# RWKV attention and a squared-ReLU FFN on one core: transposing the scaled r and k by DMA, and a second PSUM bank for FFN2

## The chip, the core and the metric

The kernel runs on one core of a Trainium2 chip. The core has a matrix engine (TensorE, PE in the profile, with its weight loads in a row of their own, PEld), three engines for elementwise work (VectorE, DVE; ScalarE, ACT; GpSimd, POOL), and SyncE (SP), which here only issues DMAs. Each engine takes its instructions in the order in which they were emitted and waits at each for what it needs. TensorE writes to PSUM, which has eight banks of 2 KB per partition; everything else lies in SBUF. DMAs are moved by 16 DMA engines and issued from SP's queue (SPq in the timeline).

The metric is the device time in microseconds of one execution. A profiled execution gives the trace that the text quotes.

## The reference

Two steps, cut to what is computed. `r`, `k`, `v` are (4, 8, 768, 48): batch, heads, time steps, head dimension.

```python
for t in range(S):                       # S = 768
    cur = einsum('bhd,bhe->bhde', u * k[t], v[t])
    y[:, :, t] = einsum('bhd,bhde->bhe', r[t], state + cur)
    state = w * state + einsum('bhd,bhe->bhde', k[t], v[t])
x = y.transpose(0, 2, 1, 3).reshape(3072, 384)
h = maximum(x @ w_in, 0)                 # w_in is 384 x 2048
out = (h * h) @ w_out                    # w_out is 2048 x 384
```

## The kernel before

**Chunks.** Time is cut into 6 chunks of 128 steps; with 4 batches that makes 24 chunks, numbered so that chunk i is time chunk i // 4 of batch i % 4. Inside a chunk the recurrence becomes matrix products. With k scaled by powers of w (`kh`) and r by their inverse counterpart (`rt`), the products of every pair of steps are A = kh times rt (transposed both), masked to the causal half and stored as `Bm`. Then Y = rt times the carried state plus Bm times v, and U = kh times v updates the state. The state of a batch is `S0W[b]`.

**Functions of a chunk.** `prep` (L201) multiplies k and r by the tables `Wkhat` and `Wt2` into `kh_buf` and `rt_buf`, four buffers each, in bf16, with heads padded from 48 to 64 columns. `prep_du` (L206) makes the product for the u term (`P`). `cast_v` (L213) casts v on ACT. `bonus` (L218) reduces P to `du` and multiplies it by v (`dv`) on DVE. `piece_T` (L229) transposes kh and rt on PE, eight transposes of 128 x 128 into one PSUM bank of pool `psT`, and one ACT copy (L239) brings them to SBUF as `rkT`. `piece_A` (L242) is eight matmuls on `rkT` into `Ap` and two DVE multiplications by the mask (L258). `piece_YU` (L261) is Y and U on PE, then `xs` = Y + dv (L288) and the state update: `ts` on DVE (L295), and `S0W` on POOL (L296). `piece_X` (L299) transposes xs on PE into a bank of `psT` and copies it to `xT` on ACT (L307).

**FFN.** Two chunks make a group g, of which there are 12. `piece_F1` (L312) computes 256 of the 2048 hidden columns for the 256 rows of a group: six matmuls into `hp` (pool `psH`, two banks), ReLU on ACT to `hr` (L326), and the square `hq` on DVE (L331), for every fourth piece on ACT (L329). The bank of `hp` is free when DVE has read it. `piece_F2` (L336) does four matmuls of one chunk's output into `o`, which lies in pool `psO` with one bank; after the fourth piece of a chunk, ACT copies it to `os` (L353) and SP stores it (L354).

**Order.** The order is written out by hand. `period(ga, g1, g2)` (L391) has eight steps; step s emits FFN1 piece s of group g1, FFN2 piece s of group g2 (steps 0 to 3 the first chunk, 4 to 7 the second), then the attention step of group ga (`att`, L356): T of the first chunk a at step 0, A of a and T of b at step 1, A of b at 2, Y and U at 3 and 4, X at 5 and 6. At step 7 the loads of chunks 2ga + 6 and 2ga + 7 are issued, from ga = 2 on `preps` (L379) emits the prep of the next group's chunks on POOL at steps 0, 2, 4 and 6. Two groups of attention go first, with prep on DVE; then the weights are cast on POOL, FFN1 of groups 0 and 1 runs alone, chunks 4 and 5 are prepared, and `period(2, None, 0)` follows. From then on each period holds attention of group g + 1, FFN1 of g and FFN2 of g - 1.

**PSUM.** The banks are psT 1, psA 2 (both halves of `Ap`), psY 1, psU 1, psH 2, psO 1: all eight.

Of the kernel before, what the change touches and what calls it, by code (L numbers as in the profile page):

```python
# [10 lines left out]
BF16 = mybir.dt.bfloat16  # L11
# [5 lines left out]
def kernel(  # L17
# [11 lines left out]
    nc = tc.nc  # L29

    B, H, S, D = r.shape
# [3 lines left out]
    DP = 64  # L35
    HP = H // 2
# [3 lines left out]
    CCH = d_model // 128  # L40
# [6 lines left out]
    const = ctx.enter_context(tc.tile_pool(name="const", bufs=1))  # L47
    stage = ctx.enter_context(tc.tile_pool(name="stage", bufs=3))
    loads = ctx.enter_context(tc.tile_pool(name="loads", bufs=7))
    work = ctx.enter_context(tc.tile_pool(name="work", bufs=3))  # L50
    hid = ctx.enter_context(tc.tile_pool(name="hid", bufs=3))

    psT = ctx.enter_context(tc.tile_pool(name="psT", bufs=1, space=bass.MemoryType.PSUM))
    psA = ctx.enter_context(tc.tile_pool(name="psA", bufs=1, space=bass.MemoryType.PSUM))
    psY = ctx.enter_context(tc.tile_pool(name="psY", bufs=1, space=bass.MemoryType.PSUM))
    psU = ctx.enter_context(tc.tile_pool(name="psU", bufs=1, space=bass.MemoryType.PSUM))
    psH = ctx.enter_context(tc.tile_pool(name="psH", bufs=2, space=bass.MemoryType.PSUM))
    psO = ctx.enter_context(tc.tile_pool(name="psO", bufs=1, space=bass.MemoryType.PSUM))

    def bcast_rows(src):  # L60
        return bass.AP(
# [13 lines left out]
    def load(i):  # L75
        if i >= N:
            return
        c, b = i // B, i % B
        rf = loads.tile([128, H, D], FP32, name=f"rf_{i}", tag="rf")
        kf = loads.tile([128, H, D], FP32, name=f"kf_{i}", tag="kf")  # L80
        vf = loads.tile([128, H, D], FP32, name=f"vf_{i}", tag="vf")
        nc.sync.dma_start(out=rf, in_=r_v[b, c])
        nc.sync.dma_start(out=kf, in_=k_v[b, c])
        nc.sync.dma_start(out=vf, in_=v_v[b, c])
        nat[i] = (rf, kf, vf)
# [18 lines left out]
    def cast_w2(s):  # L104
        t = const.tile([128, 2, d_model], BF16, name=f"W2_{s}")
        nc.gpsimd.tensor_copy(t, W2f[s])  # L106
        W2.append(t)
# [44 lines left out]
    njcol = const.tile([128, 1], FP32, name="njcol")  # L152
    nc.vector.tensor_copy(njcol, njcol_i)
    NB = 4
    rt_buf, kh_buf = [], []
    for j in range(NB):
        tr = const.tile([128, H, DP], BF16, name=f"rt_{j}")
        tk = const.tile([128, H, DP], BF16, name=f"kh_{j}")
        nc.vector.memset(tr[:, :, D:DP], 0.0)
        nc.vector.memset(tk[:, :, D:DP], 0.0)  # L160
        rt_buf.append(tr)
        kh_buf.append(tk)
    wrow = const.tile([1, 2, HP, 128], FP32, name="wrow")
    nc.vector.memset(wrow, 0.0)
    esel = const.tile([1, 2, 2 * D], FP32, name="esel")
# [34 lines left out]

    def prep(i, eng):  # L201
        rf, kf, vf = nat[i]
        eng.tensor_mul(kh_buf[i % NB][:, :, 0:D], kf, Wkhat)  # L203
        eng.tensor_mul(rt_buf[i % NB][:, :, 0:D], rf, Wt2)

    def prep_du(i, eng):  # L206
        rf, kf, vf = nat[i]
        P0 = work.tile([128, H, D], FP32, name=f"P0_{i}", tag="P0")
        eng.tensor_mul(P0, rf, kf)  # L209
        eng.tensor_mul(P0, P0, ub)  # L210
        du_in[i] = P0
# [14 lines left out]
        nc.vector.tensor_mul(dv, nat[i][2], du_b)  # L226
        dvs[i] = dv

    def piece_T(i):  # L229
        pt = psT.tile([128, 2, HP, 128], BF16, name=f"pt_{i}", tag="T")  # L230
        for j, src in ((1, kh_buf[i % NB]), (0, rt_buf[i % NB])):
            for hc in range(HP):
                nc.tensor.transpose(  # L233
                    pt[:, j, hc, :],
                    src[:, 2 * hc : 2 * hc + 2, :].rearrange("p a b -> p (a b)"),
                    identity,
                )
        rkT = work.tile([128, 2, HP, 128], BF16, name=f"rkT_{i}", tag="rkT")
        nc.scalar.copy(rkT, pt)  # L239
        rkTs[i] = rkT  # L240

    def piece_A(i):  # L242
        rkT = rkTs[i]
        Ap = psA.tile([128, 2, HP, 128], FP32, name=f"Ap_{i}", tag="A")
        Bm = work.tile([128, 2, HP, 128], BF16, name=f"Bm_{i}", tag="Bm")
        for hc in range(HP):
            for e in range(2):
                p0 = 64 * e
                nc.tensor.matmul(
                    Ap[:, e, hc, :],  # L250
                    rkT[p0 : p0 + D, 1, hc, :],
                    rkT[p0 : p0 + D, 0, hc, :],
                    start=True,
                    stop=True,
                    skip_group_check=True,
                )
        for e in range(2):
            nc.vector.tensor_mul(Bm[:, e], Ap[:, e], mask_b)  # L258
        Bms[i] = Bm

    def piece_YU(i):  # L261
        c, b = i // B, i % B
        rkT, Bm, vb = rkTs.pop(i), Bms.pop(i), vbs.pop(i)
        Y = psY.tile([128, HP, 2 * D], FP32, name=f"Y_{i}", tag="Y", padded_shape=[None, None, 128])
        for hc in range(HP):
            if c > 0:
                nc.tensor.matmul(
                    Y[:, hc, :], rkT[:, 0, hc, :], S0W[b][:, hc, :],
                    start=True, stop=False, skip_group_check=True,
                )  # L270
            for e in range(2):
                nc.tensor.matmul(
                    Y[:, hc, D * e : D * (e + 1)], Bm[:, e, hc, :], vb[:, 2 * hc + e, :],
                    start=(c == 0), stop=True, skip_group_check=True,
                )
        if c < NCH - 1:
            kh = kh_buf[i % NB]
            U = psU.tile([128, HP, 2 * D], FP32, name=f"U_{i}", tag="U", padded_shape=[None, None, 128])
            for hc in range(HP):
                nc.tensor.matmul(  # L280
                    U[:, hc, :],
                    kh[:, 2 * hc : 2 * hc + 2, :].rearrange("p a b -> p (a b)"),
                    vb[:, 2 * hc : 2 * hc + 2, :].rearrange("p a b -> p (a b)"),
                    start=True, stop=True, skip_group_check=True,
                )
        xs = work.tile([128, HP, 2 * D], BF16, name=f"xs_{i}", tag="xs")
        dv = dvs.pop(i)
        nc.vector.tensor_add(xs, Y, dv.rearrange("p (a e) d -> p a (e d)", e=2))  # L288
        xss[i] = xs
        if c < NCH - 1:  # L290
            if c == 0:
                nc.vector.tensor_mul(S0W[b], U, WLm)
            else:
                ts = work.tile([128, HP, 2 * D], FP32, name=f"ts_{i}", tag="ts")
                nc.vector.tensor_add(ts, U, S0W[b])  # L295
                nc.gpsimd.tensor_mul(S0W[b], ts, WLm)  # L296
        nat.pop(i)

    def piece_X(i):  # L299
        g, j = i // 2, i % 2  # L300
        if j == 0:
            xTs[g] = work.tile([128, CCH, GT], BF16, name=f"xT_{g}", tag="xT")
        xf = xss.pop(i).rearrange("p a b -> p (a b)")
        px = psT.tile([128, CCH, 128], BF16, name=f"px_{i}", tag="T", padded_shape=[None, 8, None])
        for c in range(CCH):
            nc.tensor.transpose(px[:, c, :], xf[:, 128 * c : 128 * (c + 1)], identity)  # L306
        nc.scalar.copy(xTs[g][:, :, L * j : L * (j + 1)], px)  # L307
# [48 lines left out]
    def att(g, s):  # L356
        a = 2 * g
        b = a + 1
        if s == 0:
            cast_v(a)  # L360
            piece_T(a)
            bonus(a)
        elif s == 1:
            piece_A(a)
            piece_T(b)
        elif s == 2:
            cast_v(b)
            piece_A(b)
            bonus(b)
        elif s == 3:  # L370
            piece_YU(a)
        elif s == 4:
            piece_YU(b)
        elif s == 5:
            piece_X(a)
        elif s == 6:
            piece_X(b)

    def preps(g, s):  # L379
        if g >= NG:  # L380
            return
        if s == 0:
            prep(2 * g, nc.gpsimd)
        elif s == 2:
            prep_du(2 * g, nc.gpsimd)
        elif s == 4:
            prep(2 * g + 1, nc.gpsimd)
        elif s == 6:
            prep_du(2 * g + 1, nc.gpsimd)

    def period(ga, g1, g2):  # L391
        for s in range(8):
            if g1 is not None:
                piece_F1(g1, s)
            if g2 is not None:
                piece_F2(g2, s)
            if ga is not None:
                att(ga, s)
                if s == 7:
                    load(2 * ga + 6)  # L400
                    load(2 * ga + 7)
                if ga > 1:
                    preps(ga + 1, s)

    for i in range(4):
        prep(i, nc.vector)
        prep_du(i, nc.gpsimd)
        if i % 2 == 1:
            period(i // 2, None, None)
    for s in range(NS):  # L410
        cast_w1(s)
    for s in range(NS):
        cast_w2(s)
    period(None, 0, None)
    period(None, 1, None)
    for i in (4, 5):
        prep(i, nc.gpsimd)
        prep_du(i, nc.gpsimd)
    period(2, None, 0)
    for g in range(2, NG + 1):  # L420
        period(g + 1 if g + 1 < NG else None, g if g < NG else None, g - 1)
# [30 lines left out]
```

## Time and profile before

| | us |
|---|---|
| median of 2 runs | 215.95 (215.7 to 216.2) |
| the profiled execution | 217.31 |
| its span in the trace | 215.6 |

| engine | busy, us |
|---|---|
| PE | 179.5 |
| DVE | 135.5 |
| ACT | 128.2 |
| POOL | 120.9 |

Busy time is the time in which an engine has an instruction in work; PE's matmuls overlap, so a busy PE is not one at its peak. The span falls into parts: the attention of the first four chunks until the first FFN1 piece at 33.2 us, FFN1 of two groups until about 51.5, a period with attention and FFN2 alone until 62.5, nine full periods of about 14.6 us until 194.5, one period of FFN1 and FFN2, and the last FFN2. The trace names its rows by tile with a running number (`rkT_1691`, `o_1940`) and the line of the kernel; "idle before" in square brackets at the end of a row is how long the engine had nothing to do before it, and what ended that time.

### The profile page before, as it was taken

The page shows a single profiled execution, that of the slowest core. Times are in us where ns is not written, and L with a number is a line of the kernel's source. Part 1 is how long each engine was busy: PE and PEld are TensorE (multiplying, and loading weights), DVE is VectorE, ACT ScalarE, POOL GpSimd, SP SyncE. Part 2 cuts the span into 40 slices and gives each one's busy share as a digit, 9 for nine tenths or more (in the row PEclk, how much of TensorE's full clock was granted, in tenths as well). Part 3 has the DMA queues.
Part 4 walks back from the last instruction along what each step waited for, and adds up shares of the span by engine and source line. Part 5 has one row for each costly group of instructions (what it writes and reads, how often), then busy time and mean ns, then how long its engine had stood idle before and what let it go on. Part 6 is the DMA issues. An engine that isn't in the chain of part 4 may idle for free.

```text
span 215.6 us, 4553 instructions
## 1 busy us (share of the span) xinstructions
PE 179.5 (83%) x1784; PEld 132.2 (61%) x1784; DVE 135.5 (63%) x234; ACT 128.2 (59%) x223; POOL 120.9 (56%) x130
## 2 busy tenths in 40 slices
PE   0853548677799999999999999999999999999963
PEld 0742335454476867767677677676677666676631
DVE  3389983445749749669389487594794864943300
ACT  4351405667356687575865875767758758765530
POOL 2486973995089593792873956928929930000000
PEclk9999999999999999999999999999999999999999
DMA  5999999996019238166093291480840010011101
GB/s 113 194 214 301 389 299 297 192 224 122 36 40 188 72 82 175 40 146 149 0 212 83 59 187 53 107 184 7 184 111 36 0 40 36 3 36 38 40 36 73
DMA packets 84021, 25.85 MB, mean 120 GB/s; under 512 B 75552, under 2 KB 84000, under 8 KB 84000
## 3 DMA queue, kind: packets, MB, share of 16 engines
q1 hardware_dynamic: 84000, 25.57, 49.2%
q8 instruction: 14, 0.23, 0.5%
q14 instruction: 7, 0.06, 0.1%
HBM read 20.84 MB, written 4.72 MB: 119 GB/s over the span
## 4 chain that ended last, share of the span: by engine, by line
PE 67%; ACT 13%; DVE 11%; issue 6%; DMA 2%; ACTq 0%
PE wl_ps L186 2%; DMA wb<-in_w_dram 2%; PE o_3324 L342 1%; PE o_3304 L342 1%; PE o_1675 L342 1%; PE o_2205 L342 1%; PE o_2470 L342 1%; PE o_1940 L342 1%; PE o_1410 L342 1%; PE o_1145 L342 1%; PE o_2960 L342 1%; PE o_3251 L342 1%; PE o_3187 L342 1%; PE o_3097 L342 1%; PE o_1295 L342 1%
## 5 line engine op out<-in xcount | busy, mean ns | idle before, releaser
L317 PEld LDWEIGHTS <-W_0_474 128*128 128x128 bf16 x72 | 7.3, 102 | 3.0 <-issue 0.9
L186 PE MATMUL wl_ps<-esel,wrow 1*128 1x96 f32 x16 | 3.7, 423 | 6.4 <-ACT wrow L178 6.4
L317 PEld LDWEIGHTS <-W_6_486 128*128 128x128 bf16 x72 | 6.7, 98 | 2.6 <-issue 1.9
L317 PEld LDWEIGHTS <-W_2_478 128*128 128x128 bf16 x72 | 6.8, 100 | 2.2 <-issue 1.3
L317 PEld LDWEIGHTS <-W_4_482 128*128 128x128 bf16 x72 | 6.5, 97 | 2.4 <-issue 1.7
L317 PEld LDWEIGHTS <-W_1_476 128*128 128x128 bf16 x72 | 7.0, 102 | 1.0
L317 PEld LDWEIGHTS <-W_3_480 128*128 128x128 bf16 x72 | 6.3, 98 | 2.1 <-issue 0.4
L186 PEld LDWEIGHTS wl_ps<-esel,wrow 1*128 1x128 f32 x16 | 3.5, 325 | 6.4 <-ACT wrow L178 6.4
L317 PEld LDWEIGHTS <-W_7_488 128*128 128x128 bf16 x72 | 6.7, 98 | 0.7
L317 PEld LDWEIGHTS <-W_5_484 128*128 128x128 bf16 x72 | 6.5, 98 | 0.7
L296 POOL TENSOR_TENSOR S0W_220<-ts_795,WLm 128x384 bf16<-128x384 f32 x1 | 1.0, 996 | 8.3 <-DVE ts_795 L295 8.3
L209 POOL TENSOR_TENSOR P_0_226<-rf_93,kf_94 128x384 f32<-128x384 f32 x1 | 1.4, 1369 | 4.2 <-DMA kf_94<-in_k_dram 4.2
L307 ACT COPY xT_451<-px_452 128x384 bf16<-128x384 bf16 x1 | 0.5, 479 | 5.0 <-PE px_452 L306 5.0
L307 ACT COPY xT_326<-px_327 128x384 bf16<-128x384 bf16 x1 | 0.5, 480 | 4.9 <-PE px_327 L306 4.9
L296 POOL TENSOR_TENSOR S0W_220<-ts_1281,WLm 128x384 bf16<-128x384 f32 x1 | 1.0, 1001 | 3.9 <-DVE ts_1281 L295 3.9
L296 POOL TENSOR_TENSOR S0W_222<-ts_1546,WLm 128x384 bf16<-128x384 f32 x1 | 1.0, 1000 | 3.9 <-DVE ts_1546 L295 3.9
L296 POOL TENSOR_TENSOR S0W_220<-ts_2341,WLm 128x384 bf16<-128x384 f32 x1 | 1.0, 1000 | 3.9 <-DVE ts_2341 L295 3.9
L296 POOL TENSOR_TENSOR S0W_222<-ts_2076,WLm 128x384 bf16<-128x384 f32 x1 | 1.0, 997 | 3.9 <-DVE ts_2076 L295 3.9
L296 POOL TENSOR_TENSOR S0W_222<-ts_2606,WLm 128x384 bf16<-128x384 f32 x1 | 1.0, 1002 | 3.8 <-DVE ts_2606 L295 3.8
L296 POOL TENSOR_TENSOR S0W_220<-ts_1811,WLm 128x384 bf16<-128x384 f32 x1 | 1.0, 1000 | 3.8 <-DVE ts_1811 L295 3.8
L106 POOL CAST W_4_498<-W2f_149 128x768 bf16<-128x768 f32 x1 | 0.8, 829 | 3.7 <-DMA W2f_149<-in_moe_w_out_dram 3.7
L233 PEld LDWEIGHTS <-kh_188 128*128 128x128 bf16 x24 | 2.0, 102 | 1.4 <-DVE kh_188 L203 0.6
(1198 smaller groups left out, 719.9 us busy)
## 6 DMA issues: line engine op xcount, KB each, us to landing
W1f_119<-in_moe_w_in_dram SPq DMA_DIRECT2D x1, 384.0 KB, 4.8
W1f_121<-in_moe_w_in_dram SPq DMA_DIRECT2D x1, 384.0 KB, 5.5
W1f_123<-in_moe_w_in_dram SPq DMA_DIRECT2D x1, 384.0 KB, 6.0
W1f_125<-in_moe_w_in_dram SPq DMA_DIRECT2D x1, 384.0 KB, 6.4
W1f_127<-in_moe_w_in_dram SPq DMA_DIRECT2D x1, 384.0 KB, 6.9
W1f_129<-in_moe_w_in_dram SPq DMA_DIRECT2D x1, 384.0 KB, 7.3
W1f_131<-in_moe_w_in_dram SPq DMA_DIRECT2D x1, 384.0 KB, 7.4
W1f_133<-in_moe_w_in_dram SPq DMA_DIRECT2D x1, 384.0 KB, 7.1
```

Source lines behind the costliest of these rows:

```text
L106: nc.gpsimd.tensor_copy(t, W2f[s])
L186: nc.tensor.matmul(wl_ps[:, hc, :], wrow[:, e, hc, :], esel[:, e, :], start=(e == 0), stop=(e == 1), skip_group_check=True,)
L209: eng.tensor_mul(P0, rf, kf)
L233: nc.tensor.transpose(pt[:, j, hc, :], src[:, 2 * hc : 2 * hc + 2, :].rearrange("p a b -> p (a b)"), identity,)
L296: nc.gpsimd.tensor_mul(S0W[b], ts, WLm)
L307: nc.scalar.copy(xTs[g][:, :, L * j : L * (j + 1)], px)
L317: nc.tensor.matmul(hp[:, fi, :], W1[s][:, c, 128 * fi : 128 * (fi + 1)], xT[:, c, :], start=(c == 0), stop=(c == CCH - 1), skip_group_chec ...
L342: nc.tensor.matmul(ops[i], hsq[g, f // 2][:, f % 2, L * j : L * (j + 1)], W2[f // 2][:, f % 2, :], start=(f == 0), stop=(f == FCH - 1), sk ...
```

## The change

The transposes of the scaled r and k move from PE to a DMA that transposes, for all but the first four chunks. `kh_buf` and `rt_buf` become one buffer `rk_buf` with both parts, so that one transfer from SBUF to SBUF does a chunk (1,024 columns of 128 rows, 256 KB). `turn(i)` takes the place of `piece_T(i)`: for the first four chunks it transposes on PE as before, into a bank of `psH`; for the others it issues the transfer from SP. It is emitted right after `prep(i)` rather than in `att`. `rkT` has four buffers in place of three.

In `att`, A of chunk a goes to step 0 and step 1 is empty. `psT` is gone: the transposes of `xs` use the bank of `psU`, and `psO` has two banks.

The loads change place too: at step 7 of a period the loads of chunks 2ga + 4 and 2ga + 5 are issued in place of 2ga + 6 and 2ga + 7, after `preps`, and only from ga = 2 on. Chunks 4 and 5 are prepared and turned ahead of FFN1 of groups 0 and 1, and the loads of chunks 6 and 7 follow them on SP.

```diff
-    psT = ctx.enter_context(tc.tile_pool(name="psT", bufs=1, space=bass.MemoryType.PSUM))
...
-    psO = ctx.enter_context(tc.tile_pool(name="psO", bufs=1, space=bass.MemoryType.PSUM))
+    psO = ctx.enter_context(tc.tile_pool(name="psO", bufs=2, space=bass.MemoryType.PSUM))
...
+        t = const.tile([128, 2, H, DP], BF16, name=f"rk_{j}")
+        nc.vector.memset(t[:, :, :, D:DP], 0.0)
+        rk_buf.append(t)
...
-        eng.tensor_mul(kh_buf[i % NB][:, :, 0:D], kf, Wkhat)
-        eng.tensor_mul(rt_buf[i % NB][:, :, 0:D], rf, Wt2)
+        eng.tensor_mul(rk_buf[i % NB][:, 1, :, 0:D], kf, Wkhat)
+        eng.tensor_mul(rk_buf[i % NB][:, 0, :, 0:D], rf, Wt2)
...
-    def piece_T(i):
...
+    def turn(i):
+        rkT = work.tile([128, 2, HP, 128], BF16, name=f"rkT_{i}", tag="rkT", bufs=4)
         rkTs[i] = rkT
+        src = rk_buf[i % NB]
+        if i < 4:
+            pt = psH.tile([128, 2, HP, 128], BF16, name=f"pt_{i}", tag="H")
+            for j in (1, 0):
+                for hc in range(HP):
+                    nc.tensor.transpose(
+                        pt[:, j, hc, :],
+                        src[:, j, 2 * hc : 2 * hc + 2, :].rearrange("p a b -> p (a b)"),
+                        identity,
+                    )
+            nc.scalar.copy(rkT, pt)
+        else:
+            nc.sync.dma_start_transpose(
+                rkT.rearrange("p j a t -> p (j a) t"), src.rearrange("p j h d -> p (j h d)")
+            )
...
-            kh = kh_buf[i % NB]
+            kh = rk_buf[i % NB][:, 1]
...
-        px = psT.tile([128, CCH, 128], BF16, name=f"px_{i}", tag="T", padded_shape=[None, 8, None])
+        px = psU.tile([128, CCH, 128], BF16, name=f"px_{i}", tag="U", padded_shape=[None, 8, None])
...
         if s == 0:
             cast_v(a)
-            piece_T(a)
+            piece_A(a)
             bonus(a)
-        elif s == 1:
-            piece_A(a)
-            piece_T(b)
...
             prep(2 * g, nc.gpsimd)
+            turn(2 * g)
...
             prep(2 * g + 1, nc.gpsimd)
+            turn(2 * g + 1)
...
-                if s == 7:
-                    load(2 * ga + 6)
-                    load(2 * ga + 7)
                 if ga > 1:
                     preps(ga + 1, s)
+                if s == 7 and ga > 1:
+                    load(2 * ga + 4)
+                    load(2 * ga + 5)
 
     for i in range(4):
         prep(i, nc.vector)
         prep_du(i, nc.gpsimd)
+        turn(i)
...
+    for i in (4, 5):
+        prep(i, nc.gpsimd)
+        turn(i)
+        prep_du(i, nc.gpsimd)
+    load(6)
+    load(7)
     period(None, 0, None)
     period(None, 1, None)
-    for i in (4, 5):
-        prep(i, nc.gpsimd)
-        prep_du(i, nc.gpsimd)
```

More of the change, by code (lines that the diff above doesn't have):

```diff
@@ L154 @@
     NB = 4
-    rt_buf, kh_buf = [], []
+    rk_buf = []
     for j in range(NB):
[L157 to L162, printed above, removed]
+        t = const.tile([128, 2, H, DP], BF16, name=f"rk_{j}")
+        nc.vector.memset(t[:, :, :, D:DP], 0.0)
+        rk_buf.append(t)
     wrow = const.tile([1, 2, HP, 128], FP32, name="wrow")
@@ L227, in bonus @@
         dvs[i] = dv
-    def piece_T(i):
[L230 to L239, printed above, removed]
-        rkTs[i] = rkT
+    def turn(i):
+        rkT = work.tile([128, 2, HP, 128], BF16, name=f"rkT_{i}", tag="rkT", bufs=4)
+        rkTs[i] = rkT
+        src = rk_buf[i % NB]
[13 more added lines that the diff above has]
+            )
     def piece_A(i):
```

## The prediction

> **What bounds the kernel now.** I read the page first, then the stretches, the chain, the timeline of one period, and SP's queue. The page gives busy time and share of each engine:
>
> ```profile
> span 215.6 us, 4553 instructions
> ...
> PE 179.5 (83%) x1784; PEld 132.2 (61%) x1784; DVE 135.5 (63%) x234; ACT 128.2 (59%) x223; POOL 120.9 (56%) x130
> ```
>
> PE leads. Stretches cut at the starts of FFN2's even chunks (busy us in the order PE, PEld, DVE, ACT, POOL; clock, DMA share, GB/s) say where:
>
> ```profile
> 107.00:121.60 14.60, 14.06 (x150) 10.51 (x150) 10.34 (x18) 10.27 (x19) 10.07 (x11) 1.00 0.50 109
> 194.50:206.10 11.60, 10.12 (x75) 7.25 (x75) 4.15 (x6) 6.53 (x12) 0.00 (x0) 1.00 0.10 36
> ```
>
> A period with attention, FFN1 and FFN2 takes 14.6 us, of which PE is busy 14.06; the last one without attention 11.6 with PE at 10.12. So PE's time and short holes bound the full periods, and a wait bounds the other. The clock granted was 1.00. The chain (start, us, what) names both:
>
> ```profile
> 107.83 0.45 PE pt_1682 L233 x8
> ...
> 111.12 0.65 PE o_1675 L342 x4
> 111.77 0.12 issue
> 111.89 0.40 PE Ap_1754 L249 x8
> ...
> 119.94 0.61 ACT hr_7_1906 L326
> ...
> 121.10 0.47 ACT os_1914 L353
> ...
> 121.62 0.81 PE o_1940 L342 x4
> ```
>
> The eight transposes of a chunk take 0.45 us of PE, A of the second chunk waits for ACT's copy, and FFN2 of the next chunk (121.62) waits until ACT has emptied the only psO bank. The timeline of this period, on ACT, DVE and POOL (start, us, operation, idle time before it):
>
> ```profile
> 108.32 1.01 ACT L239 COPY rkT_1691<-pt_1682 128x1024 bf16<-128x1024 bf16 x1 [0.45 <-PE pt_1682 L233]
> ```
>
> ```profile
> 108.11 0.54 DVE L221 TENSOR_REDUCE du_1693<-P_12_1505 128x8 f32<-128x384 f32 x1
> 108.69 0.56 DVE L226 TENSOR_TENSOR dv_1695<-vf_1124,du_1693 128x384 f32<-128x384 f32 x1
> 109.86 0.69 DVE L331 TENSOR_TENSOR hq_1_1708<-hp_1_1699,hr_1_1706 128x512 bf16<-128x512 f32 x1 [0.61 <-ACT hr_1_1706 L326]
> 110.47 1.28 DVE L258 TENSOR_TENSOR Bm_1715<-Ap_1714,maskJT 128x512 bf16<-128x512 f32 x2
> ```
>
> ```profile
> 116.00 1.00 POOL L296 TENSOR_TENSOR S0W_220<-ts_1811,WLm 128x384 bf16<-128x384 f32 x1 [3.85 <-DVE ts_1811 L295]
> ...
> 118.48 0.99 POOL L203 TENSOR_TENSOR kh_192<-kf_1394,Wkhat 128x384 bf16<-128x384 f32 x1
> 119.44 0.99 POOL L204 TENSOR_TENSOR rt_191<-rf_1393,Wt_205 128x384 bf16<-128x384 f32 x1
> ```
>
> POOL idles 3.85 us before S0W: that is its slack. SP's queue (issue time of each DMA), then two landings and the slowest load:
>
> ```profile
> 121.59 0.36 SPq L354 DMA_DIRECT2D out_dram<-os_1914  x1
> 122.04 0.39 SPq L82 DMA_DIRECT2D rf_1917<-in_r_dram  x1
> ...
> 126.86 0.84 SPq L84 DMA_DIRECT2D vf_1925<-in_v_dram  x1
> ```
>
> ```profile
> kf_144<-in_k_dram SPq DMA_DIRECT2D x1, 192.0 KB, 8.7
> ...
> out_dram<-os_1914 SPq DMA_DIRECT2D x1, 192.0 KB, 2.0
> ...
> kf_1918<-in_k_dram SPq DMA_DIRECT2D x1, 192.0 KB, 3.6
> ```
>
> **The change, part by part.** I walked the kernel from 10 us on, working out start times in emission order: each instruction starts when its engine is free and its last input is there, with the durations above, 0.65 us for an FFN piece (the chain's o pieces), and one PSUM bank handed on only when its reader is done. For the old order this gives 14.55 us a period (measured 14.60) and 213.5 us in all (215.6). I use differences of such walks only.
>
> *PE transposes and copies removed (20 chunks).* Per period PE loses twice the 0.45 us that the chain gives eight transposes (0.46 in the walk), ACT 2 x 1.01, and the 0.12 wait before A goes. ACT was not the bound, so its 2 us count only where it was waited for: in the first period with attention and FFN2 alone, where both copies stood in line before A, the walk goes from 12.1 to 10.4 us.
>
> *Two psO banks.* FFN2 no longer waits for the output copy: 0.41 us of hole and what it delays. Alone, the walk gives 14.0 us a period. In the FFN-only period the wait (FFN1, ReLU, square, copy, then FFN2) weighs more:
>
> ```profile
> 206.08 0.48 PE L342 MATMUL o_3304<-W_0_490,hq_0_3185 128*128 128x384 bf16 x2 [1.06 <-ACT os_3301 L353]
> ```
>
> The walk goes from 11.53 (measured 11.60) to 9.78 there, and loses as much as a copy and its hand-over, 0.6, before the last chunk. All this edit alone is worth 7.4 us in the old order.
>
> *A one step earlier.* Ap moves from step 1 to step 0, and on DVE Bm (1.28) now stands with du and dv (0.54, 0.56) before hq_1 and hq_2. What is late next: FFN1 piece 3 needs the bank that hq_1 frees, hq_1 ends 5.2 us after the period's start, PE is ready at 4.7: 0.55 us of new hole. Then Y of the second chunk waits 0.16 for xs, U 0.1 for ts. So the period comes to 13.54 us, not the 13.15 that subtraction gives.
>
> *px moved to psU.* px of the first chunk must wait for ts of the second: 0.07 us per period; about nothing, but in the start phase it is on the path.
>
> *Start phase.* Four chunks keep PE transposes, but now both of a group go ahead of A:
>
> ```profile
> 11.01 1.35 DVE L204 TENSOR_TENSOR rt_183<-rf_101,Wt_205 128x384 bf16<-128x384 f32 x1
> ...
> 12.24 0.61 PE L249 MATMUL Ap_251<-rkT_245 48*128 48x128 bf16 x8 [1.10 <-ACT rkT_245 L239]
> ...
> 33.16 1.49 PE L317 MATMUL hp_0_506<-xT_326,W_0_474 128*128 128x256 bf16 x6
> ```
>
> A(0), at 12.24 now, will wait for chunk 1's scaled r (11.01 + 1.35 = 12.36) and its four transposes (0.4 at the slow start): 12.8. Bm goes ahead of du and dv, so xs is 0.4 later; px waits for the second S0W product, 0.9; the second group loses the same 0.5 once more. The walk starts FFN1 at 35.3 where the old walk has 33.4 (measured 33.16): 1.9 us lost. The sixteen FFN1 pieces behind it are bound by PSUM hand-over, not by PE, so nothing is won back there.
>
> *Buffers.* One memset in place of two, rkT with four buffers: nothing, DVE waits for the first load then. Refilling an rk buffer also waits until its transfer has read it, four chunks ago.
>
> *The transfers and SP's queue.* This is the price that the trace does not show. Each turn makes SP wait for POOL's rt; behind it on SP stand the stores and, in the same period, six loads. A late store costs nothing while three os buffers last. The loads are now four chunks ahead instead of six, so they are needed at once by the next prep: POOL's 3.85 us of idle time covers that, but it closes a loop: store 0.40, r load 0.42, k landing 3.7 (row: 3.6), eight POOL operations of 0.96 (k, r, P twice, S0W twice, k, r: 7.7), two hand-overs of 0.1, and D, the time SP is held by one transfer: 12.46 + D. The second loop is that of the second chunk's transposed data: A starts 111.89, its rt ends 120.43, so 8.54 + D + X, with X from issue to landing. The period is the longest of 13.54, 12.46 + D and 8.54 + D + X. D costs nothing up to 1.1 us, D + X nothing up to 5.0.
>
> Bounds. D: from 0.36 (the store's issue) upward; six loads held SP from 122.04 to 127.70, 0.94 each, in as many row pieces (1,024) as a 256 KB transfer of 256-byte rows would have. Scaled by bytes, 0.94 x 256/192 = 1.26; I take 1.3, as the source is cut the way the loads are. D + X: from 2.0 (store) to 8.7 (a load behind weights); nearest is k's 3.6, times 256/192 that is 4.8 at most; I take 4.3, midway between 3.6 and 4.8, rounded up. DMA engines at half their share have room for the 0.5 MB more per period. An effect below nothing is excluded: a transfer can do no more than be hidden.
>
> [...]
>
> *Sum* (new walk minus old): start 1.9; first attention-and-FFN2 period -1.7; the next 13.99 for 14.55, -0.6; six at 12.46 + 1.3 = 13.76 for 14.55, -4.7; the two full periods without loads -0.9 and -1.1; the FFN-only one -1.75; last chunk -0.75. Together -9.6: 203.9 for 213.5. The profiled execution took 217.3 with a span of 215.6; the median is 215.95, and 215.95 - 9.6 = 206.3.
>
> **Rivals.**
> 1. *SP is held longer*: D of 1.7 to 2.5, each 0.1 us paid in seven or eight periods. For: all loads hang behind the turns, and loads held SP for up to twice the store's time. Against: the store's 0.36. D = 2.1 gives 210.1 in the walk, so 212.5; 2.5 gives 213.3, so 215.8. [...]
> 2. *The second chunk's data is late* (the other side): D + X above 6.9 makes it slower by 2%, from 5.0 on each us costs 8 us. At 8.7, the slowest load, the walk gives 232.7, so 235. For: nothing in the trace says that a transpose moves at a load's speed. Against: the queue is empty when it is issued, and bytes are only a third more. [...]
> 3. *The transfers are wholly hidden* (D at most 1.1, D + X below 5): period 13.54, walk 201.8, so 204.2. For: the store's 0.36. Against: loads in as many pieces hold SP for 0.94.
> 4. *The transposes buy nothing*: only psO acts, 14.0 a period, and the start's loss stays: -7.4 + 1.9, so 210.5. For: DVE, not PE, may set the period once Bm moves ahead. Against: the walk already has DVE's order in it and still gains.
>
> **How the numbers follow.** Forecast (204.5 to 209) 0.50; rival 3, 0.12; rivals 1 and 4 (209 to 215) 0.18; rival 2, 0.20. The range leaves rival 2 out: 203.5 (rival 3's 204.2 with 0.3% off) to 215. A measurement tells about 2% from no change, that is 211.6 and 220.3: faster has the forecast, rival 3 and the nearer half of 1 and 4, 0.70; within 2% the other half and a fifth of rival 2, 0.12; slower 0.18.
>
> **What would show it.** Right: no L233 rows after the fourth chunk, no wait of o pieces for os, FFN2 starts 13.5 to 13.9 apart, the FFN-only period near 9.8, DVE waits moved to hq_1. SP's row for a turn shows D, the DMA list X. Wrong: Ap of second chunks waiting for the transfer by over 1 us in every period (rival 2); kh on POOL waiting for kf beyond 4.5 us after the store (rival 1); PE below full clock, or FFN1 starting after 36 us.

## The result, and the profile after

| | before | after |
|---|---|---|
| median of 2 runs, us | 215.95 | 204.97 (204.68 to 205.26) |
| the profiled execution, us | 217.31 | 205.26 |
| its span, us | 215.6 | 203.6 |

The changed kernel takes 0.949 of the time before (95% interval 0.942 to 0.957): 11.0 us less by the medians, where 9.6 were forecast. Medians of the experiments below leave out five executions that took over 1.5% more than the fastest of the same kernel (213.25 us in experiment 2, 213.15 in 3, 210.28 in 6, 207.76 in 8, 208.7 in 10). The page of the changed kernel, with busy time by engine and the chain by engine:

```profile
span 203.6 us, 4241 instructions
...
PE 168.7 (83%) x1624; PEld 123.2 (61%) x1624; DVE 133.2 (65%) x230; ACT 109.9 (54%) x203; POOL 117.8 (58%) x130
...
PE 25%; POOL 24%; DVE 20%; DMA 13%; SPq 8%; issue 5%; ACT 4%; ACTq 0%
```

PE is busy 10.8 us less and ACT 18.3 us less, and PE's share of its own span is the same 83%. What is new stands in the last line: POOL, DMA and SP's queue carry 45% of the chain. Before, the same line of the page was

```profile
PE 67%; ACT 13%; DVE 11%; issue 6%; DMA 2%; ACTq 0%
```

Stretches of the changed kernel from one first load to the next, and the FFN-only period (busy us in the order PE, PEld, DVE, ACT, POOL; clock, DMA share, GB/s):

```profile
106.45:120.32 13.87, 13.19 (x136) 9.59 (x134) 10.48 (x19) 8.59 (x18) 9.67 (x11) 1.00 0.69 152
120.32:134.08 13.76, 12.92 (x135) 9.60 (x134) 10.37 (x19) 8.31 (x17) 9.80 (x11) 1.00 0.80 155
184.58:194.37 9.79, 9.79 (x77) 7.24 (x75) 4.15 (x6) 5.96 (x12) 0.00 (x0) 1.00 0.11 40
```

A full period takes 13.8 us for 14.6, with PE idle for 0.7 to 0.8 of it; the FFN-only period takes 9.79 for 11.60 and PE never stops in it. The chain through one period (start, us, what):

```profile
106.45 0.43 SPq L81
...
106.93 3.58 DMA kf_1562<-in_k_dram
...
110.58 1.01 POOL rk_180 L199
...
117.43 0.95 POOL rk_182 L200
118.39 0.97 POOL P_15_1787 L205
119.35 0.30 SPq L240
...
119.74 0.53 SPq L356
...
120.32 0.42 SPq L81
```

and SP's queue at its end, the issue of each DMA:

```profile
118.41 1.24 SPq L240 DMA_TRANSPOSE rkT_1744<-rk_182  x1
119.74 0.53 SPq L356 DMA_DIRECT2D out_dram<-os_1805  x1
120.32 0.42 SPq L81 DMA_DIRECT2D rf_1808<-in_r_dram  x1
```

This is the loop of the prediction: r load, k landing, eight POOL operations (110.58 to 118.39, 7.8 us), the turn, the store, the next r load. The chain books 0.97 us under P_15, which only ran beside the transfer; SP's rows show that the transfer held the queue from 118.41 to 119.65. So D is 1.24 us. One line of the DMA list (last figure: us from issue to landing), one of PE's waits and one of POOL's (total, times, longest) show where data is late:

```profile
rkT_1744<-rk_182 SPq DMA_TRANSPOSE x1, 2.7
```

```profile
PE Ap_1890 L251 <- DMA rkT_1744<-rk_182: 0.8, 1, 0.8
```

```profile
POOL rk_176 L199 <- DMA kf_1809<-in_k_dram: 3.8, 1, 3.8
```

The transfer lands 2.7 us after its issue, PE waits 0.8 us for it in this period (0.5 to 0.9 in seven periods), and POOL's idle time, formerly a wait for ts, is now a wait for k.

### The profile page after: what moved, and what is told of

Read it like the earlier page. It is cut to its first block, busy times and chain, and to the rows that moved or that the text cites. A ratio compares the mean times of both kernels' runs of the same rounds, so it can differ in the third digit from the quotient of the medians.

```text
span 203.6 us, 4241 instructions
## 1 busy us (share of the span) xinstructions
PE 168.7 (83%) x1624; PEld 123.2 (61%) x1624; DVE 133.2 (65%) x230; ACT 109.9 (54%) x203; POOL 117.8 (58%) x130
## 2 busy tenths in 40 slices
DMA packets 105140, 31.07 MB, mean 153 GB/s; under 512 B 96672, under 2 KB 105120, under 8 KB 105120
## 3 DMA queue, kind: packets, MB, share of 16 engines
q1 hardware_dynamic: 105120, 30.81, 66.3%
## 4 chain that ended last, share of the span: by engine, by line
PE 25%; POOL 24%; DVE 20%; DMA 13%; SPq 8%; issue 5%; ACT 4%; ACTq 0%
SPq L83 2%; SPq L81 2%; DMA kf_1562<-in_k_dram 2%; DMA kf_2056<-in_k_dram 2%; DMA kf_1315<-in_k_dram 2%; DMA kf_1809<-in_k_dram 2%; DMA kf_1068<-in_k_dram 2%; DMA rf_110<-in_r_dram 2%; DMA vf_828<-in_v_dram 2%; POOL rk_180 L199 1%; POOL rk_178 L199 1%; POOL rk_182 L200 1%; POOL rk_178 L200 1%; POOL S0W_211 L298 1%; POOL rk_182 L199 1%
## 5 line engine op out<-in xcount | busy, mean ns | idle before, releaser
L319 PEld LDWEIGHTS <-W_0_439 128*128 128x128 bf16 x72 | 7.3, 102 | 3.0 <-issue 0.9
L319 PEld LDWEIGHTS <-W_2_443 128*128 128x128 bf16 x72 | 7.1, 99 | 3.3 <-issue 1.3
L319 PEld LDWEIGHTS <-W_6_451 128*128 128x128 bf16 x72 | 6.6, 97 | 2.6 <-issue 1.9
L319 PEld LDWEIGHTS <-W_3_445 128*128 128x128 bf16 x72 | 6.4, 97 | 2.9 <-issue 1.2
L319 PEld LDWEIGHTS <-W_4_447 128*128 128x128 bf16 x72 | 6.5, 97 | 2.4 <-issue 1.7
L319 PEld LDWEIGHTS <-W_1_441 128*128 128x128 bf16 x72 | 6.6, 102 | 2.0
L319 PEld LDWEIGHTS <-W_7_453 128*128 128x128 bf16 x72 | 6.7, 98 | 0.7
L319 PEld LDWEIGHTS <-W_5_449 128*128 128x128 bf16 x72 | 6.5, 98 | 0.7
L199 POOL TENSOR_TENSOR rk_180<-kf_486,Wkhat 128x384 bf16<-128x384 f32 x1 | 1.0, 1007 | 4.9 <-DMA kf_486<-in_k_dram 4.9
L199 POOL TENSOR_TENSOR rk_176<-kf_821,Wkhat 128x384 bf16<-128x384 f32 x1 | 1.0, 998 | 4.6 <-DMA kf_821<-in_k_dram 4.6
L199 POOL TENSOR_TENSOR rk_180<-kf_1068,Wkhat 128x384 bf16<-128x384 f32 x1 | 1.0, 999 | 4.1 <-DMA kf_1068<-in_k_dram 4.1
L199 POOL TENSOR_TENSOR rk_180<-kf_1562,Wkhat 128x384 bf16<-128x384 f32 x1 | 1.0, 1007 | 4.0 <-DMA kf_1562<-in_k_dram 4.0
L199 POOL TENSOR_TENSOR rk_180<-kf_2550,Wkhat 128x384 bf16<-128x384 f32 x1 | 1.0, 1000 | 4.1 <-DMA kf_2550<-in_k_dram 4.1
L199 POOL TENSOR_TENSOR rk_180<-kf_2056,Wkhat 128x384 bf16<-128x384 f32 x1 | 1.0, 1002 | 4.0 <-DMA kf_2056<-in_k_dram 4.0
L199 POOL TENSOR_TENSOR rk_176<-kf_2303,Wkhat 128x384 bf16<-128x384 f32 x1 | 1.0, 1006 | 3.9 <-DMA kf_2303<-in_k_dram 3.9
L199 POOL TENSOR_TENSOR rk_176<-kf_1315,Wkhat 128x384 bf16<-128x384 f32 x1 | 1.0, 997 | 3.9 <-DMA kf_1315<-in_k_dram 3.9
L199 POOL TENSOR_TENSOR rk_176<-kf_1809,Wkhat 128x384 bf16<-128x384 f32 x1 | 1.0, 1004 | 3.8 <-DMA kf_1809<-in_k_dram 3.8
```

The source lines that it names most:

```text
L199: eng.tensor_mul(rk_buf[i % NB][:, 1, :, 0:D], kf, Wkhat)
L319: nc.tensor.matmul(hp[:, fi, :], W1[s][:, c, 128 * fi : 128 * (fi + 1)], xT[:, c, :], start=(c == 0), stop=(c == CCH - 1), skip_group_chec ...
```

## The experiments

The kernel before took 216.2 to 216.7 us (medians) beside these runs; each ratio, with its 95% interval, is against it. Line numbers are those of the kernel run, and tiles have no running numbers there.

**1. The second psO bank alone.** Is the gain due to the bank or to the transfers?

```diff
 # in the kernel before
-    psT = ctx.enter_context(tc.tile_pool(name="psT", bufs=1, space=bass.MemoryType.PSUM))
-    psO = ctx.enter_context(tc.tile_pool(name="psO", bufs=1, space=bass.MemoryType.PSUM))
+    psO = ctx.enter_context(tc.tile_pool(name="psO", bufs=2, space=bass.MemoryType.PSUM))
-        pt = psT.tile([128, 2, HP, 128], BF16, name=f"pt_{i}", tag="T")
+        pt = psU.tile([128, 2, HP, 128], BF16, name=f"pt_{i}", tag="U")
 # and px from psT to psU in the same way
```

> The kernel before with only the second psO bank; the bank comes from psT, whose transposes (of r and k, and of xs) go to psU's bank. Theory (the bank is worth the larger half): the period goes from 14.6 to 14.0 us, the FFN-only period from 11.6 to 9.8, in all 6 to 7 us less than before, 209 to 210. Rival (the gain belongs to the transfers): less than 2 us, 214 or more.

Measured: 210.87 us, ratio 0.974 (0.970 to 0.978), 5.7 us less than before. One period of it, columns as above:

```profile
107.82:121.90 14.08, 13.94 (x154) 10.52 (x152) 10.34 (x18) 10.16 (x20) 10.10 (x11) 1.00 0.52 113
```

The walk gave 14.0 us for this period. PE is busy 13.94 of 14.08: with the bank alone, PE is full. The gain lies just under the expected 6 to 7 us. That is the start: FFN1 begins at 34.32 us for 33.16 before, and 0.8 of these 1.2 us come from px, which in psU's bank waits for S0W (from the second group's xs to FFN1 there are 3.54 us for 2.70). From FFN1's start to the end of the span the two traces have 182.4 us before and 174.9 here: 7.6 us less, of which up to 0.7 may be that the execution traced before was slow beside the others (217.31 for a median of 216.56).

**2. The changed kernel with one psO bank.**

```diff
-    psO = ctx.enter_context(tc.tile_pool(name="psO", bufs=2, space=bass.MemoryType.PSUM))
+    psO = ctx.enter_context(tc.tile_pool(name="psO", bufs=1, space=bass.MemoryType.PSUM))
```

> The changed kernel with one psO bank, one bank left empty. Theory (the loop of loads, POOL and SP sets the period): full periods stay at 13.8 us and only the periods without loads and the end lose, 3 to 4 us in all, 208 to 209. Rival (the periods are bound by PE and its banks): 0.4 to 0.6 us in each of 11 periods, 210 to 212.

Measured: 210.57 us (209.62 to 212.04), ratio 0.974 (0.967 to 0.980), 6.0 us less than before. PE's timeline (idle time and its releaser in brackets):

```profile
118.60 0.81 PE L344 MATMUL o<-W,hq 128*128 128x384 bf16 x4 [0.41 <-ACT os L355]
...
123.12 0.40 PE L251 MATMUL Ap<-rkT 48*128 48x128 bf16 x8 [0.67 <-DMA rkT<-rk]
```

The hole of 0.41 is back, yet full periods with loads take 13.92 us in the mean, hardly more than 13.8: the loop already waits about as long. Of the 5.4 us by which the span is longer than the changed kernel's, 1.35 have arisen by the first loads of a full period (66.37 for 65.02), 0.9 arise from there to the last ones (163.83 for 161.59), and 3.2 after them. The 1.35 are not the bank's: FFN1 starts 1.5 us later here, at 34.25 for 32.76, by the same code and before any output bank is in use (experiment 6 comes back to this). So in the changed kernel the bank is worth about 4 us, most of it behind the last loads, where the loop through the loads does not run. That is the theory's 3 to 4 us; the time lies above its 208 to 209, in the rival's range, because of the start.

The two parts do not add up. From FFN1's start to the end of the span the traces, one of each kernel, have 182.4 us before, 174.9 with the bank alone, 174.8 with the rest of the change alone and 170.8 with both: gains of 7.6, 7.7 and 11.6.

**3. The loads one group earlier.** If the loop through the loads sets the period, taking the loads out of it should bring the walk's 13.54.

```diff
-                    load(2 * ga + 4)
-                    load(2 * ga + 5)
+                    load(2 * ga + 6)
+                    load(2 * ga + 7)
...
-    load(6)
-    load(7)
+    for i in range(6, 10):
+        load(i)
```

> The changed kernel with loads six chunks ahead, as before the change (loads 8 and 9 go with 6 and 7). Theory (loop of loads): POOL no longer waits for k, the period falls from 13.8 to the 13.5 of PE and DVE, 1.5 to 2 us less than the changed kernel, 203. Rival (PE and DVE set 13.8 already): no change, 205.

Measured: 210.05 us (209.86 to 210.32), ratio 0.971 (0.967 to 0.975): 4 to 5 us slower than the changed kernel (204.97, and 206.03 in experiment 10). Both expectations fall. DVE's rows, then POOL's, at the start of a period:

```profile
106.09 1.28 DVE L260 TENSOR_TENSOR Bm<-Ap,maskJT 128x512 bf16<-128x512 f32 x2
...
120.29 1.28 DVE L260 TENSOR_TENSOR Bm<-Ap,maskJT 128x512 bf16<-128x512 f32 x2
121.48 0.54 DVE L217 TENSOR_REDUCE du<-P 128x8 f32<-128x384 f32 x1
122.06 1.22 DVE L222 TENSOR_TENSOR dv<-vf,du 128x384 f32<-128x384 f32 x1
123.20 1.27 DVE L333 TENSOR_TENSOR hq<-hp,hr 128x512 bf16<-128x512 f32 x2
```

```profile
121.86 1.00 POOL L205 TENSOR_TENSOR P<-rf,kf 128x384 f32<-128x384 f32 x1
122.94 1.19 POOL L206 TENSOR_TENSOR P<-P,ub 128x384 f32<-128x384 f32 x1
```

The period is 14.20 us (106.09 to 120.29). dv takes 1.22 where 0.56 was assumed, and ends only after POOL's product, which began 0.2 before it, is done; POOL's next product then takes 1.19 for 1.00. dv stands ahead of hq_1 on DVE, hq_1 frees the bank for FFN1 piece 3, and so the 0.66 us go straight into the period: 13.54 + 0.66 = 14.20. In the changed kernel POOL's last product ends while this dv runs (at 120.42, dv from 119.93; rows in the last section), and then POOL stands idle for its k load. The late loads, which looked like a cost, kept POOL out of DVE's way for the most part.

**4. Each transfer twice**, the second into a buffer that nobody reads, to price D: it adds one more hold of SP and 256 KB per chunk.

```diff
+            again = work.tile([128, 2, HP, 128], BF16, name=f"again_{i}", tag="again", bufs=4)
+            nc.sync.dma_start_transpose(
+                again.rearrange("p j a t -> p (j a) t"), src.rearrange("p j h d -> p (j h d)")
+            )
```

> The changed kernel with each transfer issued twice, the second into a buffer that nobody reads. Theory (loop of loads, 12.46 + D): SP is held 1.24 us longer ahead of the loads, periods of 15.0 to 15.1, in seven of them, 9 us in all, 213 to 215. Rival (SP's time is hidden, only A's wait for its data counts): the real transfer is issued first, so 207 or less.

Measured: 217.34 us, ratio 1.003 (1.000 to 1.007): the whole gain is gone. SP's queue:

```profile
113.00 0.42 SPq L81 DMA_DIRECT2D rf<-in_r_dram  x1
...
124.96 1.24 SPq L240 DMA_TRANSPOSE rkT<-rk  x1
126.25 1.29 SPq L244 DMA_TRANSPOSE again<-rk  x1
127.64 0.53 SPq L360 DMA_DIRECT2D out_dram<-os  x1
128.22 0.42 SPq L81 DMA_DIRECT2D rf<-in_r_dram  x1
```

The period is 15.22 us here (113.00 to 128.22) and 15.26 in the mean, 1.46 more than in the changed kernel. 1.29 of it is the second hold of SP, so time on SP's queue is paid in full: the loop binds. A of the second chunk now waits up to 2.3 us for its data, but the chain of this period does not go that way: it runs from the r load over k's landing, eight POOL operations, both transfers and the store to the next r load, without a piece of PE. The time lies above the expected 213 to 215: seven periods at 1.46 make 10.2 us, and FFN1 starts 1.4 us later than in the changed kernel's trace (34.15 for 32.76), which is no effect of this edit (experiment 6).

**5. Each transfer twice, with the loads earlier** (the edits of 3 and 4). If the doubled transfer costs through the loop, it should cost next to nothing with the loads out of the loop; if through traffic, as much as before.

> Each transfer issued twice, and loads six chunks ahead. Theory (SP's time counts only through the loop of loads): with the loads ahead the doubled hold of SP is free, so the time is that of the run with the loads earlier alone, 210, within 1.5. Rival (the doubled transfers cost by their traffic or by SP's time as such): 214 to 217, as with the loads late.

Measured: 212.63 us, ratio 0.981 (0.976 to 0.985), 2.6 us more than experiment 3, where doubling cost 11 to 12 in experiment 4: 1.1 us outside what the theory allowed, and below the rival's 214. Bm of the first chunk in two periods running, then PE at the first transposed data:

```profile
109.84 1.28 DVE L264 TENSOR_TENSOR Bm<-Ap,maskJT 128x512 bf16<-128x512 f32 x2
...
124.04 1.28 DVE L264 TENSOR_TENSOR Bm<-Ap,maskJT 128x512 bf16<-128x512 f32 x2
```

```profile
65.05 0.61 PE L255 MATMUL Ap<-rkT 48*128 48x128 bf16 x8 [3.03 <-DMA rkT<-rk]
```

The period is 14.20 us, to the hundredth that of experiment 3: in the steady state the second transfer is free. What it costs falls in one place, a wait of 3.03 us before the first full period (0.39 there in experiment 3).

**6. The start in its old order** (for the first four chunks, the turn of a at step 0 and its A at step 1, with the turn of b). The prediction put a loss of 1.9 us on the new order.

```diff
         if s == 0:
             cast_v(a)
-            piece_A(a)
+            if a < 4:
+                turn(a)
+            else:
+                piece_A(a)
             bonus(a)
+        elif s == 1 and a < 4:
+            piece_A(a)
+            turn(b)
...
-        turn(i)
```

> The changed kernel, but the first four chunks are transposed inside the attention steps, in the order of before (first chunk at step 0, A of it and the second chunk's transposes at step 1). The prediction's term (the new order of the start costs 1.9 us): FFN1 starts at about 31 us and the time falls by 1.9, to 203. Rival (what the two traces show, FFN1 at 33.0 and 33.2): no change, 205 within 0.7.

Measured: 205.22 us (205.08 to 207.17), ratio 0.950 (0.945 to 0.956): as the rival had it. Of PE's timeline, px of the second group's first chunk and the first FFN1 piece in the changed kernel, then the FFN1 piece here, then in experiment 2, whose start is that of the changed kernel:

```profile
31.45 0.48 PE L308 MATMUL px_429<-identity,xs_408 128*128 128x128 bf16 x3 [0.68 <-DVE S0W_212 L294]
...
32.76 1.49 PE L319 MATMUL hp_0_497<-xT_315,W_0_439 128*128 128x256 bf16 x6
```

```profile
34.23 0.64 PE L319 MATMUL hp<-xT,W 128*128 128x256 bf16 x2
```

```profile
34.25 0.63 PE L319 MATMUL hp<-xT,W 128*128 128x256 bf16 x2
```

FFN1 does not start 1.9 us earlier in the old order. It starts 1.5 later than in the changed kernel's trace, but that is not the order's doing either: over the nine traces with the new order (the changed kernel, experiments 2 to 5 and 7 to 10) the same code starts FFN1 anywhere from 32.76 to 34.30 us, at 34.01 in the median. Experiments 2 and 6 can be compared directly, as DVE's preparation of the second group takes 4.39 us in both (3.45 in the changed kernel's trace): 34.25 with the new order, 34.23 with the old. So the new order, beside the other edits, costs nothing that shows.

**7. The U-term products of POOL left out for even chunks from the fourth on**, with the loads of experiment 3. The u term of these chunks is thus missing. POOL is then free while DVE does dv; if POOL was what lengthened dv, the period must come to 13.54.

```diff
+    noP = const.tile([128, H, D], FP32, name="noP")
+    nc.vector.memset(noP, 0.0)
...
     def prep_du(i, eng):
+        if i >= 4 and i % 2 == 0:
+            du_in[i] = noP
+            return
```

> Loads six chunks ahead; POOL's two products for the u term are left out for the even chunks from 4 on (their u term is zero), so POOL is idle while DVE multiplies v by du of the first chunk. Theory (that multiplication takes 1.22 us instead of 0.56 because POOL reads two SBUF inputs beside it): it goes back to 0.56, the period from 14.2 to 13.5 to 13.6, the time to 203 to 205. Rival (the order on DVE alone makes 14.2): no change, 210.

Measured: 204.61 us, ratio 0.944 (0.941 to 0.948). DVE's rows:

```profile
104.73 1.28 DVE L266 TENSOR_TENSOR Bm<-Ap,maskJT 128x512 bf16<-128x512 f32 x2
...
106.50 0.56 DVE L228 TENSOR_TENSOR dv<-vf,du 128x384 f32<-128x384 f32 x1
...
118.27 1.27 DVE L266 TENSOR_TENSOR Bm<-Ap,maskJT 128x512 bf16<-128x512 f32 x2
```

dv is back at 0.56 and the period is 13.54 us, the walk's figure. The contention is shown, and with it the first bound of the prediction.

**8. Four squares on ACT, loads as in the changed kernel.** ACT does the squares of FFN1 pieces 1, 2, 3 and 7 rather than 3 and 7, so that dv no longer stands ahead of hq_1 and hq_2. This takes away the order of DVE, but not the loop through the loads.

```diff
-        if s % 4 == 3:
+        if s in (1, 2, 3, 7):
```

> The changed kernel with the four squares on ACT, but with its loads four chunks ahead as it has them. Theory (two bounds of nearly the same length, the loop of loads at 12.46 + 1.24 and DVE's order): with DVE relieved the loop of loads alone stays, periods of 13.7, the time 203 to 204.5, hardly better than the changed kernel. Rival (DVE's order was the only bound): 13.0 and 201, as with the loads earlier.

Measured: 205.01 us (203.86 to 206.44), ratio 0.948 (0.943 to 0.954): no clear gain on the changed kernel, which took 206.03 beside it (0.952, 0.949 to 0.955). POOL's waits from 95 to 160 us:

```profile
POOL rk L199 <- DMA kf<-in_k_dram: 19.2, 5, 4.0
```

POOL still waits up to 4 us for k in each period, and the loop of the loads keeps the period at 13.69, the expected 13.7 (first loads from 94.96 to 163.39, five periods).

**9. Both: four squares on ACT and the loads one group earlier.**

> Loads six chunks ahead, and the squares of FFN1 pieces 1, 2, 3 and 7 on ACT instead of 3 and 7, so that DVE has 1.4 us less in each period, early, and PSUM banks 1 and 2 are freed by the ReLU. Theory (with the loads early, DVE's order sets the period of 14.2, lengthened by its contention with POOL): the period falls to 13.0, the time to 197 to 200. Rival (DMA traffic or PE holds 14 us): 207 or more.

Measured: 201.05 us, ratio 0.927 (0.924 to 0.931), 3.9 us below the changed kernel's first timing and well clear of it. One period:

```profile
101.99:115.00 13.01, 13.01 (x136) 9.60 (x135) 9.62 (x16) 9.70 (x18) 9.92 (x11) 1.00 0.77 163
```

PE is busy for all of its 13.01 us. The period is the expected one; the time lies 1 us above the expected 197 to 200, with FFN1 starting at 34.30. Either edit alone gains nothing clear (8) or loses 4 to 5 us (3); together they gain, since the changed kernel had two bounds of nearly the same length.

**10. The changed kernel again**, beside the kernel before and experiment 8.

> The changed kernel itself, beside the run above on the same chip, so that the two can be compared: 205 within 0.7, FFN1 from 33 us, periods of 13.8.

Measured: 206.03 us (205.40 to 206.82), ratio 0.952 (0.949 to 0.955). Together with the first 204.97 this says how far a median moves from one session to the next: about 1 us. FFN1 starts at 32.78; the one trace is of the execution of 208.7 us, so it says nothing on the expected period of 13.8.

## Why the prediction was right, and where its sizes were off

The time, 206.3 forecast for 204.97, and the mechanism held: a gain from both parts, limited by a loop through SP's queue. The terms of the sum, against the starts of FFN2's even chunks in both traces:

| term | forecast, us | measured, us |
|---|---|---|
| start, to FFN2 at 51.14 before, 50.74 after | +1.9 | -0.4 |
| first attention-and-FFN2 period, 11.91 to 11.17 | -1.7 | -0.7 |
| the next, 14.78 to 13.32 | -0.6 | -1.5 |
| six periods of 13.76 forecast | -4.7 | -4.9 |
| two full periods without loads | -0.9, -1.1 | -1.3, -1.1 |
| FFN-only period, 11.57 to 9.79 | -1.75 | -1.8 |
| last chunk | -0.75 | -0.3 |
| sum | -9.6 | -12.0 |

The sum of 12.0 is that of the two spans, 215.6 to 203.6; the profiled execution before lay 1.4 us above its median and the one after 0.3, so the medians show 11.0. Apart from the start, the terms add up to 11.5 forecast and 11.6 measured. That they come so near is in part luck: the first two periods are off by 1.0 and 0.9 us in opposite directions.

**The loop: right.** D was taken as 1.3 from the loads' 0.94 us for as many row pieces; it is 1.24. The pages count 84,000 packets on queue q1 before and 105,120 after, 1,056 more for each of the 20 transfers, near the 1,024 assumed. The forecast period was 12.46 + 1.3 = 13.76 (the terms of the 12.46, as printed, add up to 12.42); the first loads of eight groups are issued from 65.02 to 161.59, 13.80 apart. D came out a little shorter and the store's issue a little longer (0.53 for 0.36 to 0.40), which nearly cancel. Experiment 4 shows that SP's time is paid in full, experiment 5 that it is free once the loads are off the loop. Rival 1 (D of 1.7 or more) and rival 3 (D at most 1.1) are refuted by the same row.

**The data's landing: right in its effect, mis-sized.** D + X was taken as 4.3 and is 2.7 to 2.8 for the second chunk of a group (3.2 once). Since up to 5.0 was free, the error cost nothing. A of the second chunk does wait 0.8 us for its data, as the turn itself comes late in the loop, but the chain does not run through that wait. Rival 2 is refuted.

**The psO bank: right.** 7.4 us were forecast alone. Experiment 1 shows 6.9 to 7.6 from FFN1's start on, with the period right (14.08 for 14.0), and 5.7 in the medians, as its start is later. Rival 4, that the transposes buy nothing, is refuted by experiment 2: with one bank the rest of the change is worth 6.0 us.

**The start: wrong.** The steps "xs is 0.4 later" and "the second group loses the same 0.5 once more" came out smaller than forecast, and the term was off by 2.3 us in these two traces, the largest error of the sum. DVE's preparation of the second group, and its first xs, before and after:

```profile
20.32 1.13 DVE L203 TENSOR_TENSOR kh_188<-kf_108,Wkhat 128x384 bf16<-128x384 f32 x1
21.38 1.17 DVE L204 TENSOR_TENSOR rt_187<-rf_107,Wt_205 128x384 bf16<-128x384 f32 x1
...
23.57 1.17 DVE L204 TENSOR_TENSOR rt_191<-rf_113,Wt_205 128x384 bf16<-128x384 f32 x1
...
30.46 0.55 DVE L288 TENSOR_TENSOR xs_431<-Y_417,dv_374 128x384 bf16<-128x384 f32 x1
```

```profile
19.98 0.80 DVE L199 TENSOR_TENSOR rk_180<-kf_105,Wkhat 128x384 bf16<-128x384 f32 x1
20.70 0.55 DVE L200 TENSOR_TENSOR rk_180<-rf_104,Wt_194 128x384 bf16<-128x384 f32 x1
...
22.26 1.17 DVE L200 TENSOR_TENSOR rk_182<-rf_110,Wt_194 128x384 bf16<-128x384 f32 x1
...
29.23 0.55 DVE L290 TENSOR_TENSOR xs_408<-Y_394,dv_374 128x384 bf16<-128x384 f32 x1
```

From the end of the second group's preparation to its xs there are 5.7 us before (24.74 to 30.46) and 5.8 after (23.43 to 29.23): the new order loses 0.1 us there, not 0.5 (0.1 to 0.6 in the nine traces of experiment 6, 0.2 in the median). Only px's wait came as forecast: from that xs to FFN1 there are 2.70 us before and 3.53 after, 0.83 more for the forecast 0.9 (0.68 of it in px's row of experiment 6). Against it stands the preparation itself, which is 0.95 us quicker after (0.33 and 0.62 in these rows), while POOL's weight casts beside it fell at other times (that they are the cause was not tried apart); the walk kept the slow durations. So from the first scaled r (11.01 before, 10.57 after) to FFN1 there are 22.15 us before and 22.19 after, and the 0.4 us gained is the earlier first load. This is luck of the one execution: in experiment 2, with the same start, the preparation is slow, and it is 23.62 us (10.63 to 34.25). By the median of the nine traces, 34.01 against the one trace before, 33.16, the start costs 0.9 us, about half of the forecast 1.9. The prediction quoted 1.35 us for the first scaled r, while the product just before it, of the same shape, took 0.56 in the same trace; that spread was not asked about.

**The first period: too large by 1.0 us.** Here too an operation of DVE met one of POOL (DVE, then POOL, after):

```profile
53.70 1.36 DVE L222 TENSOR_TENSOR dv_694<-vf_142,du_692 128x384 f32<-128x384 f32 x1
```

```profile
53.64 1.01 POOL L205 TENSOR_TENSOR P_6_726<-rf_485,kf_486 128x384 f32<-128x384 f32 x1
```

dv started just after a product of POOL and took 1.36, 0.8 more than the walk's 0.56. That it costs the period the same 0.8 was not tried, nor is it known why the next period gained 0.9 more than forecast.

**POOL's 3.85 us of slack: a reading that was too simple.** The prediction took this idle time as mere cover for the late loads. Experiments 3 and 7 show that it does a second thing: while POOL waits, DVE's dv runs undisturbed. And the two bounds, 13.54 from the order of DVE and 13.70 from the loop, were taken as separate; with dv at 0.59 to 1.00 in six of the first seven full periods of the changed kernel they are of about one length, and neither edit of 3 and 8 alone gained clearly.

What stays open: why the last chunk gained 0.3 and not 0.75 us, and whether the store's issue of 0.53 us comes from the transfers ahead of it on the queue (the last six stores, with none ahead, take 0.33).

## What to carry to other kernels

When work moves from a busy engine to a DMA, ask what stands behind the DMA on the queue that issues it: here 1.24 us of issue per transfer, not the 2.7 us of its landing, set the period, because the next loads stood behind it. Before loads are moved earlier to break such a loop, ask what the idle time that they cause protects; with two bounds of one length, both must go (experiment 9), and either alone shows little or a loss. In a walk with fixed durations, an operation that has two different durations in the trace is a question to settle first. And before a difference between two traces is put down to an edit, look at a stretch that the edit does not touch: here the start of the same code differed by 1.5 us from run to run.

## What the runs showed of the hardware

- **dv on DVE took longer beside a product of POOL.** dv, which reads two SBUF tensors, took 0.56 us alone and 1.22 or 1.36 when POOL had started a product 0.20 or 0.06 before it; in both cases it ends 0.4 us after POOL's product. With POOL idle beside it in experiment 7 it took 0.56 (106.50). Squares that read one input from PSUM did not take longer beside POOL (two in 1.27 us, at 123.20 in experiment 3, while POOL ran at 122.94; two in 1.28 with POOL idle, at 120.76 in the changed kernel). The changed kernel shows the middle case, DVE and then POOL:

```profile
119.93 0.90 DVE L222 TENSOR_TENSOR dv_1852<-vf_1563,du_1850 128x384 f32<-128x384 f32 x1
```

```profile
119.42 1.00 POOL L206 TENSOR_TENSOR P_15_1787<-P_15_1787,ub 128x384 f32<-128x384 f32 x1
```

  dv starts halfway through POOL's product, loses 0.34, and ends 0.41 after it once more.
- **A transposing transfer of 256 KB between SBUF tiles** held SP's queue for 1.23 to 1.26 us in 15 of the changed kernel's 20 (up to 1.96 in the others) and landed 2.7 to 2.8 us after its issue in 15 of them; of the other five, at 3.2 to 4.4, four were the first transfer behind a group's loads, while others in that place took 2.7 to 2.8. In experiment 4 a second one straight behind held the queue for 1.29.
